# A runtime bound from row squares on ScalarE in place of Gram matrices on TensorE, with its last steps at another place and the whole order written anew

## The chip, the cores and the metric

The kernel runs on one core of a Trainium2 chip. The metric is the device time of one execution in microseconds (us), the median over runs. A core has five engines that run their own instruction queues in order: TensorE (PE; its weight loads are listed apart as PEld), VectorE (DVE), ScalarE (ACT), GpSimd (POOL), and SyncE (SP), which here issues the DMA transfers. [...]

## The reference, cut to what matters

Block-sparse attention over 4 batches, 8 heads, 768 positions and 64 columns a head, then an MLP whose activation is h times cos(h):

```python
def _attn_ref(q, k, v, sampled_blocks):
    scores = scale * np.matmul(q, k.transpose(0, 1, 3, 2))
    mask = np.abs(blk_i - blk_j) <= window           # own block and its neighbours, 32 positions a block
    mask = mask | (blk_i == 0) | (blk_j == 0) | (blk_i == n_blocks - 1) | (blk_j == n_blocks - 1)
    # and 3 drawn blocks for each block of queries
    scores = np.where(mask, scores, -1000000000.0)
    attn = np.exp(scores - np.max(scores, axis=-1, keepdims=True))
    attn = attn / (np.sum(attn, axis=-1, keepdims=True) + 1e-09)
    return np.matmul(attn, v)

def _moe_ref(x, w_in, w_out):      # x: 3072 x 512, w_in: 512 x 2048, w_out: 2048 x 512
    h = x @ w_in
    g = h * np.cos(h)
    return g @ w_out
```

## The kernel before, in words

**Tiling.** A batch has six query tiles of 128 rows: five sparse ones and one dense one (first and last block of the sequence among its rows). So there are 24 tiles, n = 0 to 23. Two tiles make one block of the MLP, m = 0 to 11.

**Attention, `attend(n)`.** For each unit of heads: scores on PE (`qk`, lines L1345 and L1356), masked maximum on DVE (`mx`, L1371), exponential on ACT (`ex`, L1393), a split of the result into a high and a low f16 part (`ph` on ACT, L1410; `pl` on DVE, L1414), a transpose by DMA into the tile PT (`PT`, L1434), and the product with V on PE (`pv`, L1445 and L1460). When all heads of a tile are there, DVE normalises into an f32 tile from the four `ot` buffers (`no`, L1482), ACT and DVE split it into f16 halves (`xh`, L1484; `xl`, L1486), and a DMA transposes these into `xT` (L1489). For one early tile PE transposes instead.

**MLP, `feed_forward(m)`.** 16 groups of 12 matmuls make h (`m{m}_{p}_{c}`, the first projection, L1626), ACT takes the cosine straight from PSUM (`sin`, L1643), DVE multiplies (`gm`, L1649), ACT and DVE split (`gh`, L1711; `gl`, L1714), and 16 groups of 6 matmuls make the output (`d{m}_{p}_{t}_{half}`, the second projection, L1723). ACT scales it out of PSUM (`o`, L1742) and SP stores it (`st`, L1747).

**The bound.** The sine table is used without reducing its argument, which is only right while h stays small. So the kernel works out a bound on h as it runs. Before the change each block m of x gives a Gram matrix on PE: 8 matmuls of 128x128 on `xT` (`xg{m}`, `x_gram`, L1658) into one of the two `ph` buffers in PSUM, which the first projection uses too. DVE takes its largest entry (`xr{m}`, `x_norm`, L1661). At the very end DVE scales and reduces these (`ba`, `bound_a`, L1667 and L1668), PE spreads the result over the partitions with one matmul (`bs`, L1113), and DVE multiplies by the weights' norms and compares (`bb`, `bound_b`, L1116 and L1674 to L1678). All five engines then load this flag into a register (L1681) and branch (L1769): over a second, general program that follows in the instruction stream, or into it. On these inputs the general program isn't run.

**Order.** A planner (`plan_kernel`) creates 3327 operations, each with its engine and its reads and writes. The table `POS` gives each its place: operations are issued in the order of these numbers, one in-order queue for each engine, with buffers handed out in that same order. So the table decides what stands behind what on every engine. With it stand `PARAMS` and the nominal costs, which decide nothing while the table covers every operation.

Of the kernel before, what the change touches and what calls it, by code (L numbers as in the profile page):

```python
# [16 lines left out]
ALU = mybir.AluOpType  # L17
# [3 lines left out]
P = 128  # L21
# [174 lines left out]
]  # L196


# [1611 lines left out]
```

## Time and profile before

| | |
|---|---|
| median of 3 runs | 787.79 us (785.78 to 788.1) |
| the profiled execution's own time | 788.36 us |
| its span, first to last instruction | 786.6 us |
| PE busy | 678.8 us (86%) |
| ACT busy | 597.9 us (76%) |
| DVE busy | 565.0 us (72%) |
| mean share of the 16 DMA engines, queue q1 | 85.5% |

Busy shares are averages over stages with different limits. A line of a group names the source line, the engine, the operation, what it writes and reads with shapes, a count, the busy time, the mean of one in ns, and after the second bar the idle time of that engine just before these instructions, with what ended it. A row of stages has the stretch, its length, then the busy us of PE, PEld, DVE, ACT and POOL with the number of instructions in brackets, TensorE's granted clock, the DMA engines' share and GB/s. A line of waits names who waited, for whom, and then the total, the number of times and the longest. The chain of waits follows the work that ended last back from the end, in order of time.

### The profile page before, as it was taken

Reading aid. Unit: us, or ns where it says so; the run is one execution under the profiler, and the core shown is the slowest. Engines: PE = TensorE matmul, PEld = TensorE weight load, DVE = VectorE, ACT = ScalarE, POOL = GpSimd, SP = SyncE. Lnnn points to the kernel's source line nnn. Section 1 sums busy time; section 2 is a strip of 40 time slices with the busy share of each in tenths; the row PEclk is TensorE's granted clock in tenths of the full one; section 3 lists DMA queues with packets and bytes.
Section 4 is the critical chain, followed back from the end, with each engine's and each line's share of the span. In section 5 each row is a group of like instructions: output and inputs, shape, how many; then the busy total and the mean of one; then the engine's idle time right before and its main releaser. Section 6 shows DMA issues by size and latency. Waiting matters only on the chain.

```text
span 786.6 us, 26927 instructions
## 1 busy us (share of the span) xinstructions
PE 678.8 (86%) x10953; PEld 473.1 (60%) x10953; DVE 565.0 (72%) x1646; ACT 597.9 (76%) x1216; POOL 17.1 (2%) x42
## 2 busy tenths in 40 slices
PE   2354459788998898999999999999999899999995
PEld 2333347566576556666676667667667576766762
DVE  5999989889788787757986677767874655464222
ACT  1867788889958988979888889878998666675321
POOL 5300000000000000000000000000000000000000
PEclk9855559999999999999999999999999999999998
DMA  9899997989999999998998999998998968644100
GB/s 311 251 275 223 188 263 172 199 205 213 256 187 215 170 183 186 176 212 186 201 181 199 197 184 195 229 184 141 185 190 176 171 128 177 120 83 78 54 1 31
DMA packets 243572, 141.11 MB, mean 179 GB/s; under 512 B 203376, under 2 KB 203504, under 8 KB 243440
## 3 DMA queue, kind: packets, MB, share of 16 engines
q1 hardware_dynamic: 243440, 139.32, 85.5%
q8 instruction: 87, 1.43, 0.8%
q14 instruction: 45, 0.37, 0.2%
HBM read 77.67 MB, written 12.58 MB: 115 GB/s over the span
## 4 chain that ended last, share of the span: by engine, by line
PE 40%; DVE 18%; DMA 17%; ACT 12%; issue 6%; SPq 6%; DVEq 1%; ACTq 0%
PE ph L1626 17%; PE po L1723 16%; DMA PT<-ring 5%; ACT P L1393 3%; DMA W<-kn 3%; DMA V<-scr 3%; DVE P L1371 3%; DVE ring L1414 2%; PE sp L1345 2%; SPq L1307 2%; DMA w<-in_moe_w_out_dram 2%; PE xp L1445 2%; ACT ring L1410 2%; DMA w<-in_moe_w_in_dram 1%; DMA U<-n 1%
## 5 line engine op out<-in xcount | busy, mean ns | idle before, releaser
L1626 PE MATMUL ph<-xT,w 128*128 128x256 f16 x2304 | 270.1, 275 | 4.7 <-DMA xT<-n 2.7
L1723 PE MATMUL po<-w,g 128*128 128x512 f16 x1152 | 263.7, 379 | 5.5 <-issue 2.9
L1626 PEld LDWEIGHTS <-w 128*128 128x128 f16 x2304 | 224.0, 99 | 44.2 <-DMA xT<-n 3.7
L1723 PEld LDWEIGHTS <-g 128*128 128x128 f16 x1152 | 110.4, 98 | 125.4 <-issue 5.4
L1393 ACT ACTIVATE P<-P,sm 128x256 f32<-128x256 f32 (+1 forms) x224 | 139.2, 622 | 19.0 <-DVE sm L1388 13.0
L1414 DVE TENSOR_TENSOR ring<-P,ring 128x512 f16<-128x512 f32 (+1 forms) x144 | 87.8, 625 | 37.7 <-ACT ring L1410 36.7
L1643 ACT ACTIVATE g<-ph,sm 128x512 f32<-128x512 f32 x96 | 72.3, 773 | 41.7 <-PE ph L1626 41.2
L1649 DVE SCALAR_TENSOR_TENSOR hs<-ph,sm,g 128x512 f32<-128x512 f32 x80 | 58.7, 747 | 50.4 <-ACT g L1643 50.0
L1410 ACT CAST ring<-P 128x512 f16<-128x512 f32 (+1 forms) x144 | 78.2, 566 | 15.5 <-DMA PT<-ring 13.7
L1345 PE MATMUL sp<-W,U 128*32 128x192 f16 (+1 forms) x2560 | 57.9, 240 | 23.4 <-DVE sm L1371 11.1
L1714 DVE TENSOR_TENSOR g<-hs,g 128x1024 f16<-128x1024 f32 x48 | 58.6, 1221 | 21.5 <-ACT g L1711 21.5
L1371 DVE CUSTOM_DVE_ANT_1 P<-sp,bias 128x256 f32<-128x256 f32 x160 | 61.8, 419 | 16.5 <-PE sp L1345 15.1
L1345 PEld LDWEIGHTS <-U 128*32 128x32 f16 x2560 | 45.8, 106 | 38.6 <-issue 29.8
L1711 ACT ACTIVATE g<-hs 128x1024 f16<-128x1024 f32 x48 | 50.4, 1051 | 12.5 <-DVE hs L1649 12.0
L1445 PE MATMUL xp<-V,PT 128*32 128x64 f16 x3840 | 41.5, 201 | 14.5 <-DMA PT<-ring 6.2
L1445 PEld LDWEIGHTS <-PT 128*32 128x32 f16 x3840 | 36.9, 97 | 24.2 <-issue 14.6
L1393 ACT ACTIVATION_READ_ACCUMULATOR P<-P,sm 128x1 f32 x224 | 41.8, 187 | 0.0
L1643 ACT ACT_TABLE_LOAD x30 | 38.5, 1283 | 0.5
L1371 DVE CUSTOM_DVE_ANT_1 P<-sp,dbias 128x384 f32<-128x384 f32 x64 | 34.4, 548 | 5.7 <-PE sp L1356 4.7
L1393 ACT ACT_TABLE_LOAD x29 | 37.2, 1283 | 0.9 <-DVE sm L1388 0.4
L1174 ACT COPY W<-W 128x256 f16 (+1 forms) x112 | 33.8, 377 | 5.3 <-issue 3.3
L1356 PE MATMUL sp<-W,U 128*128 128x384 f16 x128 | 29.6, 329 | 2.7 <-DVE sm L1371 2.2
(155 smaller groups left out, 644.5 us busy)
## 6 DMA issues: line engine op xcount, KB each, us to landing
V<-scr SPq DMA_DIRECT2D x40, 384.0 KB, 5.0
V<-scr SPq DMA_DIRECT2D x240, 64.0 KB, 3.5
w<-in_moe_w_in_dram SPq DMA_DIRECT2D x12, 512.0 KB, 6.0
stage<-in_k_dram SPq DMA_DIRECT2D x12, 512.0 KB, 6.2
w<-in_moe_w_out_dram SPq DMA_DIRECT2D x12, 512.0 KB, 6.7
V<-scr SPq DMA_DIRECT2D x8, 768.0 KB, 6.7
scr<-n SPq DMA_DIRECT2D x21, 256.0 KB, 3.9
qs<-in_q_dram SPq DMA_DIRECT2D x20, 256.0 KB, 3.9
```

What stands on the lines that cost most here:

```text
L1345: mm(o, U[:, z, h, rows], k, start=(a == 0 and z == 0 and part == 0), stop=(a == 1 and z == 1 and part == 1), tile_position=(0, BLK * j),)
L1371: self.nc.vector.tensor_tensor_reduce(out=self.head_cols(n, a, Pt).rearrange("p (n c) -> p n c", c=BLK), in0=self.head_cols(n, a, sp).rear ...
L1393: self.nc.scalar.activation(Pv, Pv, AF.Exp, scale=qc[:, 4:5], bias=nb[:, bcol : bcol + 1], accum_out=sums[:, 2 * j + a : 2 * j + a + 1],)
L1410: self.nc.scalar.copy(hi, p)
L1414: self.nc.vector.tensor_tensor(lo, p, hi, ALU.subtract)
L1445: mm(xp[32 * j : 32 * j + 32, h, :], PT[:, 4 * a + 2 * l + c, 32 * j : 32 * j + 32], V[:, j, c, h, d0:d1], start=(a == 0 and c == 0 and x ...
L1626: self.nc.tensor.matmul(ph[:, ff, :], self.W1[p][:, wl, cc, c * P : (c + 1) * P], xT[:, xl * NCC + cc, :], start=(j == 0), stop=(j == len( ...
L1643: self.nc.scalar.activation(self.half_cols(g, h), ph.rearrange("p f t -> p (f t)"), AF.Sin, scale=self.turns[b][:, p : p + 1], bias=self.h ...
L1649: self.nc.vector.scalar_tensor_tensor(self.half_cols(hs, h), ph.rearrange("p f t -> p (f t)"), c, self.half_cols(g, h), op0=ALU.mult, op1= ...
L1711: self.nc.scalar.activation(g[:, 0:1024], hs, AF.Copy)
L1714: self.nc.vector.tensor_tensor(g[:, 1024:2048], hs, g[:, 0:1024], ALU.subtract)
L1723: self.nc.tensor.matmul(po, g[:, gl, ff, t * P : (t + 1) * P], self.W2[p][:, wl, ff, :], start=(first and ff == half * hf and j == 0), sto ...
```

## The change

Instead of the Gram matrices, ACT squares each normalised f32 tile as soon as the order lets it, and adds along the row (`xs{n}`, `x_square`, 24 of them, one column each). The steps `ba`, `bs` and `bb` keep their arithmetic, on 6 columns a batch in place of 3. The order table is replaced as a whole: 3327 numbers again, since 24 operations go and 24 come. Two of its lines stand here.

```diff
 POS = [
-    2, 3, 5, 16, 4, 15, 9, 11, 10, 6, 39, 32, 46, 29, 48, 40, 49, 52, 57, 59, 60, 61, 62, 126, 245, 351, 154, 272, 353, 329, 73, 1091, 327, 956, 1387,
+    5, 8, 26, 9, 24, 144, 6, 7, 23, 25, 101, 10, 18, 11, 27, 12, 28, 29, 31, 32, 34, 35, 36, 180, 43, 456, 191, 62, 281, 160, 37, 976, 226, 1276,
...
     xTs = {}
+    xgs = []
...
         op("ACT", 0.525, np_ + 0.01, lambda: f(3), r=[y], w=[(xn, 0)], name=f"xh{n}")
+        if not general:
+            xgs.append(Val())
+            op("ACT", 0.613, np_ + 0.02, lambda: e.x_square(n, y.t), r=[y], w=[xgs[-1]], name=f"xs{n}")
         op("DVE", 0.602, np_ + 0.01, lambda: f(4), r=[y, (xn, 0)], w=[(xn, 1)], name=f"xl{n}")
...
-    xgs = []
-
     def feed_forward(m):
         b = seq[m * TT][0]
-        if not general:
-            gr, xg = Val("ph"), Val()
-            xgs.append(xg)
-            op("PE", 0.46, m * TT * CYC, lambda: e.x_gram(xTs[m].t, gr.t), r=[xTs[m]], w=[gr], name=f"xg{m}")
-            op("DVE", 0.21, m * TT * CYC, lambda: e.x_norm(m, gr.t), r=[gr], w=[xg], name=f"xr{m}")
...
-        self.xnorm = self.col(len(self.seq) // self.TT)
+        self.xnorm = self.col(len(self.seq))
...
-    def x_gram(self, xT, g):
-        n = self.TT * self.NCC
-        for k in range(n):
-            r, c = divmod(k, self.NCC)
-            x = xT[:, c, r * P : r * P + P]
-            self.nc.tensor.matmul(self.gram_view(g), x, x, start=(k == 0), stop=(k == n - 1))
-
-    def x_norm(self, m, g):
-        self.nc.vector.tensor_reduce(self.xnorm[:, m : m + 1], self.gram_view(g), AX.X, ALU.max)
+    def x_square(self, n, y):
+        self.square(self.xnorm[:, n : n + 1], y)

     def bound_a(self):
-        nc, n = self.nc, len(self.seq) // self.TT // self.B
+        nc, n = self.nc, len(self.seq) // self.B
```

`square` is `activation(junk, src, Square, accum_out=acc)`, the same helper (L1068) that squares q and the later k and v tiles.

Three places of the new order matter below. The first is DVE's end of the program. In the version before, behind the last block's products and splits (L1649, L1714), stand the last Gram reduction and the steps `ba` and `bb`:

```order
L1649 SCALAR_TENSOR_TENSOR hs_81<-ph_116,sm,g_84 128x512
L1714 TENSOR_TENSOR g_84<-hs_81,g_84 128x1024
L1661 TENSOR_REDUCE sm<-ph_117 128x1
L1667 TENSOR_SCALAR sm<-sm 128x3 x4
L1668 TENSOR_REDUCE sm<-sm 128x1
L1116 TENSOR_REDUCE sm<-sp_112 128x1
L1674 TENSOR_TENSOR sm<-sm 128x1
L1676 TENSOR_TENSOR sm<-sm 128x1 x2
L1677 TENSOR_SCALAR sm<-sm 128x1
L1678 TENSOR_SCALAR sm<-sm 128x1
L1681 TENSOR_LOAD sm
L1769 COMPARE_AND_BRANCH
```

Of the changed kernel, DVE at the place where the last tile is normalised (there L1479 is `no23`, L1483 `xl23`, L1657 and L1658 `ba`, L1113 to L1668 `bb`, L1646 the last block's products; the numbers are three to ten lower than before):

```order
L1704 TENSOR_TENSOR g_84<-hs_81,g_84 128x1024
L1477 RECIPROCAL sm<-sm 128x8
L1479 TENSOR_TENSOR ot_108<-xp_115,sm 128x512
L1483 TENSOR_TENSOR n_89<-ot_108,n_89 128x512
L1657 TENSOR_SCALAR sm<-sm 128x6 x4
L1658 TENSOR_REDUCE sm<-sm 128x1
L1113 TENSOR_REDUCE sm<-sp_112 128x1
L1664 TENSOR_TENSOR sm<-sm 128x1
L1666 TENSOR_TENSOR sm<-sm 128x1 x2
L1667 TENSOR_SCALAR sm<-sm 128x1
L1668 TENSOR_SCALAR sm<-sm 128x1
L1646 SCALAR_TENSOR_TENSOR hs_82<-ph_116,sm,g_85 128x512
```

`ba` and `bb` moved from behind the last split of the program to ahead of all products of the last block. On PE the matmul `bs` moved with them: from the last row of the program to a place with 6 groups of the second projection of m = 10 and the whole of m = 11 (16 and 16 groups) still behind it, and 3 groups of 6 matmuls between it and `pv23_5`, the last product with V.

ACT at the same place, in the version before (L1484 is `xh23`, L1711 `gh`, L1742 the outputs of m = 10):

```order
L1643 ACTIVATE g_84<-ph_116,sm 128x512
L1484 CAST n_90<-ot_109 128x512
L1711 ACTIVATE g_84<-hs_81 128x1024
L1742 ACTIVATE ot_110<-po_119,sm 128x512
L1742 ACTIVATE ot_108<-po_118,sm 128x512
```

and in the changed one (L1481 is `xh23`, L1065 the squares of tiles 22 and 23, L1701 `gh`):

```order
L1640 ACTIVATE g_84<-ph_117,sm 128x512
L1701 ACTIVATE g_84<-hs_81 128x1024
L1481 CAST n_89<-ot_108 128x512
L1065 ACTIVATE junk,sm<-ot_111 128x512
L1065 ACTIVATE junk,sm<-ot_108 128x512
L1732 ACTIVATE ot_109<-po_119,sm 128x512
```

Two squares now stand between `xh23` and the outputs of m = 10, and `ba` waits for the second of them.

SP's last rows before, where ot_109 is tile 23 (stored in two parts) and the last ot_110 is tile 22:

```order
L1747 DMA out_dram<-ot_111 128x512
L1747 DMA out_dram<-ot_109 96x512
L1747 DMA out_dram<-ot_109 32x512
L1747 DMA out_dram<-ot_110 128x512
L1681 TENSOR_LOAD sm
L1769 COMPARE_AND_BRANCH
```

and now, where ot_108 is tile 22 and ot_110 tile 23:

```order
L1737 DMA out_dram<-ot_109 128x512
L1737 DMA out_dram<-ot_108 128x512
L1737 DMA out_dram<-ot_110 96x512
L1737 DMA out_dram<-ot_110 32x512
L1671 TENSOR_LOAD sm
L1759 COMPARE_AND_BRANCH
```

The tile with two stores is now the last one, so SP issues two transfers and not one behind the last output.

## Rows read from the trace of the kernel before

**Rows 1.** Busy time by stage: length; engines; granted TensorE clock, DMA share, GB/s.
```profile
0.00:140.00 140.00, 73.73 (x1634) 57.96 (x1635) 125.07 (x345) 97.76 (x204) 17.06 (x42) 0.70 0.92 241
140.00:640.00 500.00, 466.87 (x7808) 321.71 (x7807) 376.23 (x1160) 422.69 (x888) 0.00 (x0) 1.00 0.98 190
640.00:740.00 100.00, 100.00 (x1258) 68.60 (x1257) 51.36 (x120) 66.58 (x112) 0.00 (x0) 1.00 0.57 116
740.00:778.00 38.00, 37.93 (x258) 24.69 (x255) 10.13 (x13) 10.70 (x13) 0.00 (x0) 1.00 0.03 7
```

**Rows 2.** Waits of PE, 140 to 778 us: total, times, longest.
```profile
PE xp L1445 <- DMA V<-scr: 3.4, 4, 2.2
PE xp L1460 <- DMA PT<-ring: 3.0, 4, 1.3
...
PE ph L1626 <- DVE sm L1661: 0.5, 1, 0.5
```

**Rows 3.** End of the chain of waits: start, us, what.
```profile
765.82 11.65 PE po L1723 x54
777.48 0.46 PE ph L1658 x8
...
778.25 0.78 DVE sm L1667 x4
...
779.28 0.24 PE sp L1113
...
780.58 0.15 DVE sm L1678
```

**Rows 4.** The flag's load, line L1681: ns, first and last start.
```profile
L1681 SPq TENSOR_LOAD <-sm x1: 279/279/279, 780.8 to 780.8; - x1
```

**Rows 5.** The branch, line L1769, and the semaphore steps behind it.
```profile
L1769 SPq EVENT_SEMAPHORE  x9: 17/17/17, 784.2 to 784.8; - x9
L1769 PEldq COMPARE_BRANCH  x1: 4177/4177/4177, 781.4 to 781.4; - x1
L1769 PEldq EVENT_SEMAPHORE  x1: 51/51/51, 785.6 to 785.6; - x1
```

**Rows 6.** Tile ot, 770 to 787 us: the last outputs and stores.
```profile
L1747 SPq DMA_DIRECT2D out_dram<-ot x3: 332/350/426, 774.3 to 778.2; - x3
L1742 ACT ACTIVATE ot<-po,sm x2: 687/687/687, 773.6 to 777.5; 128x512 f32<-128x512 f32 x2
```

**Rows 7.** Groups by line: the parts that go.
```profile
L1658 PE MATMUL ph<-xT 128*128 128x128 f16 x96 | 7.3, 219 | 0.1
L1661 DVE TENSOR_REDUCE sm<-ph 128x1 f32<-128x128 f32 x12 | 3.4, 284 | 7.5 <-PE ph L1658 7.5
```

**Rows 8.** Line L1658, 640 to 700 us.
```profile
L1658 PE MATMUL ph<-xT x8: 219/219/220, 699.4 to 699.8; 128*128 128x128 f16 x8
```

**Rows 9.** ACT in order of time: a square of 128x512 and its neighbours.
```profile
311.88 0.62 ACT L1068 ACTIVATE junk<-stage 128x512 bf16<-128x512 f32 x1
...
312.49 0.76 ACT L1643 ACTIVATE g<-ph,sm 128x512 f32<-128x512 f32 x1
```

**Rows 10.** Groups by line: all loads of ACT's function tables.
```profile
L1643 ACT ACT_TABLE_LOAD x30 | 38.5, 1283 | 0.5
L1393 ACT ACT_TABLE_LOAD x29 | 37.2, 1283 | 0.9 <-DVE sm L1388 0.4
L1068 ACT ACT_TABLE_LOAD x1 | 1.3, 1283 | 0.7 <-PEq L1786 0.7
```

**Rows 11.** Line L1484, the high half of every tile: ns, first and last start.
```profile
L1484 ACT CAST n<-ot x24: 601/617/621, 91.7 to 727.5; 128x512 f16<-128x512 f32 x24
```

**Rows 12.** Sum over 160 to 200, 250 to 300 and 550 to 600 us.
```profile
sum 140.00, PE 130.96 PEld 91.50 DVE 113.79 ACT 128.93 POOL 0.00; mean PE 43.65 PEld 30.50 DVE 37.93 ACT 42.98 POOL 0.00
```

**Rows 13.** In order of time: PE behind the last product with V, and xh23.
```profile
726.57 9.23 PE L1723 MATMUL po<-w,g 128*128 128x512 f16 x42
...
727.50 0.62 ACT L1484 CAST n<-ot 128x512 f16<-128x512 f32 x1 [4.21 <-DVE ot L1482]
```

More of the change, by code (lines that the diff above doesn't have):

```diff
@@ L871 @@
     KD, KX = 384, 1152
-    SMALL = 296 + 72 + 24
+    SMALL = 296 + 72 + 40
     kv = wc = None
```

260 rows, old and new, of the table POS are left out of this document.

## The prediction

> **What bounds the kernel now.** I read the busy time by stage first [rows 1]. Up to 140 us PE works 73.73 us of 140 while DVE works 125.07: the start hangs on DVE and on what feeds it. From 140 to 640 PE has 466.87 of 500, ACT 422.69, and the DMA engines are taken to 0.98; three resources lie close together, and PE is idle for 33.1 us in all. From 640 to 778 PE has no idle time to speak of (100.00 of 100, then 37.93 of 38). So the end is set by PE's work, except where in the first 640 us something else leaves it idle. Next I read what PE waits for between 140 and 778 us [rows 2]: small pieces, the two largest groups 3.4 and 3.0 us, both on DMAs of the attention. Last I read the end of the chain of waits [rows 3]: the second projection ends at 777.48 us, then come the last Gram matrix and a string of small DVE steps up to the flag at 780.73, and only then the flag's loads and the branch [rows 4, 5]. The span ends at 786.6, 9.12 us behind the last useful matmul.
>
> **The tail.** Before, the flag is loaded from 780.8 on, SP's load being the row shown [rows 4]; PE's branch starts at 781.4 and takes 4.18 us, its semaphore step stands at 785.6 [rows 5], and 1.0 us later the span ends. SP is a little quicker: from its load at 780.8 to its last semaphore step at 784.8 are 4.0 us. In the changed kernel the flag is there long before, and each engine goes to its load when its own queue is through. With T for the end of the last matmul: ACT's output takes 0.69 us, and SP has two stores behind it, 0.35 and 0.33 us [rows 6], with some 0.1 us between them, so SP's load starts at T + 1.45 and its last step is at T + 5.45. PE's load starts at T, its step at T + 4.8. With the same 1.0 us behind the later one the span ends at T + 6.45. Against 9.12 that is **−2.6 us**, the last Gram matrix (0.46 us) within it. What stays is the branch, which no edit touches.
>
> The row shows 4.18 us for PE's branch and nearly as long from SP's load to its steps [rows 4, 5]. [...] I go by the rows.
>
> **The Gram matrices in the body.** 96 matmuls go [rows 7]. In the chain 8 of them take 0.46 us [rows 3], so the other eleven are 11 x 0.46 = 5.1 us. Only one of the eleven lies behind 640 us, where PE is full [rows 8]; the other ten lie where PE has idle time to swallow them. I take all of it, **−5.1 us**, since most of that idle time is short waits inside a full queue; the lower bound is one, −0.5 us. With them goes their hold on one of the two PSUM buffers of the first projection, which cost PE one wait of 0.5 us on DVE's reduction [rows 2]: **−0.5 us**. The 12 reductions themselves free 3.4 us of DVE [rows 7], which is under 80% busy behind 140 us [rows 1]; I count nothing, and at most those 3.4.
>
> **The squares.** A square of this size holds ACT's queue, with the read of its accumulator, for 0.61 us, from its start to that of the next instruction [rows 9]; 24 are 14.6 us. Counted in the two orders, the loads of ACT's tables fall from 60 to 58, 2 x 1.28 us [rows 10]: 12.1 us net. From 140 to 640 ACT is idle for 77.3 us [rows 1], which can hide them all; nothing hides them where ACT is nearly full. A tile is finished every (727.5 − 91.7) / 23 = 27.6 us [rows 11]. The three fullest stretches make 140 us, with ACT busy for 128.9 of them, 92% [rows 12], so 140 / 27.6 = 5.1 squares fall there: 5.1 x 0.61 = **+3.1 us**. The bounds are 0 and 12.1. Behind each square wait the exponentials and the cosines, and behind those DVE and PE.
>
> A square also keeps one of the four ot buffers until it has run, and the squares of tiles 0 and 1 stand far behind in ACT's new order. I cost this at nothing, because the other buffers cover it; if they don't, the nearest row is PE's longest single wait in the first group, 2.2 us [rows 2].
>
> **The wait that is added.** The matmul `bs` now stands in the middle of PE's queue, with everything of m = 11 behind it, so each us it waits is a us of the end. It needs `ba`, which needs the squares of tiles 22 and 23. From where PE turns from the last product with V to other work, 726.57, to the start of `xh23`, 727.50, DVE's product between them, are 0.93 us, `xh23` takes 0.62 [rows 13], the two squares 1.22, and from `ba` to the spreading matmul it is 779.28 − 778.25 = 1.03 [rows 3]: 3.8 us. PE has 18 matmuls to do in between, at 11.65 / 54 us each [rows 3]: 3.9 us. So it is just covered; with the matmul's own 0.24 us [rows 3] and a little lateness **+0.5 us**. The bounds are 0.2 and, without cover, 4.0.
>
> **The order.** All 3327 numbers are new. What that does the rows of before can't show. They bound it: the two largest groups of PE's waits, 6.4 us [rows 2], can be lost or come once more. I take 0 and keep ±6.4. The first 140 us are in this too, since nothing else of the change acts there.
>
> **The sum.** −2.6 − 5.1 − 0.5 + 3.1 + 0.5 = −4.6 us. It is made against the profiled execution, 788.36 us (1.8 us more than its span), and gives 783.8 there. That execution lies 0.6 us above the median of 787.79, so I forecast **783.2 us**.
>
> **Rivals.**
> - *The attention sets the pace up to 640 us.* DMA at 0.98 speaks for it, and PE's largest waits are on DMAs. Then the ten early Gram matrices only become idle time of PE, and the squares hide too: 787.79 − 2.6 − 0.5 (the Gram matrix at 699) + 0.5 = 785.2. Against it: PE is 93% busy there.
> - *ACT becomes the bound* (slower). Place: 140 to 640 us, where ACT is 85% busy and every square stands in one queue with exponentials and cosines. Price: all 12.1 us reach the end, −2.6 − 5.1 − 0.5 + 0.5 + 12.1 = +4.4, so 792.2. It makes the kernel slower than before once more than 7.7 / 0.61, about 13 squares, delay the end. For it: the 92% of the three stretches. Against it: 77.3 us idle, and two loads fewer.
> - *The new order is better or worse than the old by itself.* 783.2 ± 6.4: 776.8 or 789.6. For it: all is moved. Against it: the parts that the rows can follow, near the end, are laid out with about the same covers.
> - *The flag is not ready in time*, so `bs` holds PE as long as the old tail took: 783.2 + 2.6 = 785.8. The 3.8 us against 3.9 speak for it, the bound of 4.0 against much more.
> - *The squares switch ACT's tables.* 24 loads of 1.28 us would be 31 us more, some 814. The rows show loads at the cosine and the exponential, and a single one at the squares' line [rows 10], whose squares of q, k and v stand all through the program; the order holds two loads fewer. [...]
>
> **How the numbers follow.** The forecast 0.42, with its own range of 780 to 785.4; the attention's pace 0.18; ACT as the bound 0.13; the order worse 0.14, better 0.10; the flag late 0.02; the tables 0.01. A measurement of this kernel tells about 0.3% from no change, 2.4 us: below 785.4 is faster, above 790.2 slower. Faster: 0.42, half of the attention's case (it lies on the edge), and 0.10, together 0.61. Same: the other 0.09, 0.10 of the worse order, 0.02 of the late flag and 0.01 of ACT's case, 0.22. Slower: 0.12 of ACT's case, 0.04 of the order's, 0.01 for the tables, 0.17. The range reaches from 777.0 (no square on the path and half of 6.4 won: 783.2 − 3.1 − 3.2) to 790.5, which takes in the worse order whole and leaves most of ACT's case out.
>
> **What would show it.** The tail: the distance from the last second projection to the end of the span should be 6.5 us, with no DVE step in it. The body: PE's busy time should fall by about 7 us, and its idle time between 140 and 640 us stay near 33; if that idle time grows by 5 us, the attention sets the pace. ACT: 24 squares at 0.61 us, 58 loads, and no stretch at which PE waits longer for a cosine or exponential; ACT above 95% over a stretch would show the second rival. `bs`: a wait of PE at that matmul under half a us. The start: the first product of the first projection at about the same time; a shift of some us there is the order's doing. The forecast is wrong if the last matmul doesn't end some 2 us or more ahead of 777.48.

## The result and the profile after

The changed kernel takes 781.73 us (median of 8 runs, 778.12 to 783.65) against 788.51 us for the kernel before, run beside it (8 runs, 785.78 to 792.12): a ratio of 0.9904, with a 95% interval of 0.9876 to 0.9932. The interval lies below 1, so the changed kernel is faster, by 0.7 to 1.2%. The forecast was 783.2 us, 4.6 less than before; the profiled executions stand at 782.21 and 788.36, 6.2 apart, and their spans at 780.4 and 786.6. Ratios, here and below, leave out executions in the chip's slower state, one of which (827.1 us) is in the median given for e5. Line numbers of the changed kernel are 3 to 10 lower: L1623 is the first projection, L1713 the second, L1442 and L1457 the products with V, L1110 the spreading matmul, L1671 the flag's load, L1759 the branch.

Busy time by stage in the changed kernel, with the columns of [rows 1], the last stretch up to the end of the second projection:

```profile
0.00:140.00 140.00, 70.65 (x1623) 56.81 (x1624) 124.14 (x345) 97.63 (x207) 15.32 (x42) 0.73 0.93 244
140.00:640.00 500.00, 467.14 (x7784) 319.72 (x7783) 378.32 (x1158) 430.09 (x925) 0.00 (x0) 1.00 0.97 191
640.00:740.00 100.00, 100.00 (x1243) 68.92 (x1242) 50.18 (x122) 70.58 (x122) 0.00 (x0) 1.00 0.53 106
740.00:774.00 34.00, 33.50 (x214) 20.57 (x211) 9.22 (x10) 8.56 (x11) 0.00 (x0) 1.00 0.01 4
```

PE is idle for 69.35 us in the start (66.27 before), for 32.86 us from 140 to 640 (33.13 before) and not at all behind that. The first product of the first projection starts at 119.0 us in place of 116.9. The end of the chain of waits, and then the flag's load, the branch and the stores by line (ns, first and last start):

```profile
752.78 20.73 PE po L1713 x96
773.51 0.02 issue
773.54 0.69 ACT ot L1732
```

```profile
L1671 PEldq TENSOR_LOAD <-sm x1: 489/489/489, 769.5 to 769.5; - x1
...
L1671 SPq TENSOR_LOAD <-sm x1: 579/579/579, 775.1 to 775.1; - x1
...
L1759 SPq EVENT_SEMAPHORE  x9: 17/17/17, 778.5 to 779.1; - x9
...
L1759 PEldq COMPARE_BRANCH  x1: 3421/3421/3421, 770.1 to 770.1; - x1
L1759 PEldq EVENT_SEMAPHORE  x1: 51/51/51, 773.5 to 773.5; - x1
...
L1737 SPq DMA_DIRECT2D out_dram<-ot x3: 332/332/418, 773.0 to 774.6; - x3
```

The second projection ends at 773.51 us, 3.97 earlier than in [rows 3], and the span ends 6.89 us behind it in place of 9.12. No DVE step stands there any more. PE's load (769.5) and its branch (770.1) lie ahead of 773.51: its instruction queue runs on while the last matmuls are still at work. SP, with its stores ahead of it, is the last.

The squares and ACT's table loads by line, and the spreading matmul:

```profile
L1640 ACT ACT_TABLE_LOAD x29 | 37.2, 1283 | 0.5
...
L1390 ACT ACT_TABLE_LOAD x28 | 35.9, 1283 | 0.4
...
L1065 ACT ACTIVATE junk<-ot 128x512 bf16<-128x512 f32 x24 | 14.9, 620 | 0.2
...
L1065 ACT ACT_TABLE_LOAD x1 | 1.3, 1283 | 0.7 <-PEq L1776 0.7
```

```profile
L1110 PE MATMUL sp<-ident,sm x1: 219/219/219, 723.8 to 723.8; 128*128 128x128 f16 x1
its engine sat idle before it (us, times) until:
who waited for it (us, times):
  DVE sm L1113: 0.7, 1
```

24 squares of 0.62 us, 58 loads, and no idle time of PE ahead of the spreading matmul. The high half of the tiles starts later and ends earlier than in [rows 11], at 99.0 against 91.7 us and at 720.9 against 727.5.

### The profile page after: what moved, and what is told of

Its sections match the earlier page's. It is cut to its first block, busy times and chain, and to the rows that moved or that the text cites. A ratio compares the mean times of both kernels' runs of the same rounds, so it can differ in the third digit from the quotient of the medians.

```text
span 780.4 us, 26779 instructions
## 1 busy us (share of the span) xinstructions
PE 671.3 (86%) x10857; PEld 466.0 (60%) x10857; DVE 561.9 (72%) x1634; ACT 607.1 (78%) x1262; POOL 15.3 (2%) x42
## 3 DMA queue, kind: packets, MB, share of 16 engines
q8 instruction: 87, 1.43, 0.8%
## 4 chain that ended last, share of the span: by engine, by line
PE 38%; DVE 19%; DMA 19%; ACT 13%; issue 6%; SPq 4%; DVEq 0%; ACTq 0%
PE ph L1623 16%; PE po L1713 15%; DMA PT<-ring 8%; ACT P L1390 4%; DVE ring L1411 3%; DMA W<-kn 2%; DVE P L1368 2%; DMA qs<-in_q_dram 2%; PE sp L1342 2%; PE xp L1442 2%; ACT ring L1407 2%; SPq L1304 2%; DMA U<-n 2%; PE sp L1353 1%; DVE hs L1646 1%
## 5 line engine op out<-in xcount | busy, mean ns | idle before, releaser
L1623 PE MATMUL ph<-xT,w 128*128 128x256 f16 x2304 | 267.4, 273 | 6.6 <-DVE hs L1646 4.4
L1713 PE MATMUL po<-w,g 128*128 128x512 f16 x1152 | 265.7, 381 | 4.1 <-issue 3.8
L1623 PEld LDWEIGHTS <-w 128*128 128x128 f16 x2304 | 223.2, 98 | 46.7 <-issue 8.5
L1713 PEld LDWEIGHTS <-g 128*128 128x128 f16 x1152 | 109.6, 98 | 126.4 <-issue 7.2
L1646 DVE SCALAR_TENSOR_TENSOR hs<-ph,sm,g 128x512 f32<-128x512 f32 x80 | 59.4, 747 | 47.3 <-ACT g L1640 46.4
L1342 PE MATMUL sp<-W,U 128*32 128x64 f16 (+1 forms) x2560 | 55.5, 238 | 30.1 <-DVE sm L1368 20.1
L1342 PEld LDWEIGHTS <-U 128*32 128x32 f16 x2560 | 44.0, 104 | 45.0 <-issue 39.9
L1704 DVE TENSOR_TENSOR g<-hs,g 128x1024 f16<-128x1024 f32 x48 | 58.6, 1220 | 14.1 <-ACT g L1701 13.7
L1701 ACT ACTIVATE g<-hs 128x1024 f16<-128x1024 f32 x48 | 50.3, 1049 | 13.6 <-DVE hs L1646 13.6
L1442 PE MATMUL xp<-V,PT 128*32 128x64 f16 x3840 | 40.8, 199 | 4.0 <-DMA PT<-ring 1.9
L1442 PEld LDWEIGHTS <-PT 128*32 128x32 f16 x3840 | 36.4, 96 | 13.0 <-issue 8.9
L1732 ACT ACTIVATE ot<-po,sm 128x512 f32<-128x512 f32 x20 | 13.4, 677 | 33.6 <-PE po L1713 33.6
```

The lines of the kernel that those rows point to most:

```text
L1342: mm(o, U[:, z, h, rows], k, start=(a == 0 and z == 0 and part == 0), stop=(a == 1 and z == 1 and part == 1), tile_position=(0, BLK * j),)
L1442: mm(xp[32 * j : 32 * j + 32, h, :], PT[:, 4 * a + 2 * l + c, 32 * j : 32 * j + 32], V[:, j, c, h, d0:d1], start=(a == 0 and c == 0 and x ...
L1623: self.nc.tensor.matmul(ph[:, ff, :], self.W1[p][:, wl, cc, c * P : (c + 1) * P], xT[:, xl * NCC + cc, :], start=(j == 0), stop=(j == len( ...
L1646: self.nc.vector.scalar_tensor_tensor(self.half_cols(hs, h), ph.rearrange("p f t -> p (f t)"), c, self.half_cols(g, h), op0=ALU.mult, op1= ...
L1701: self.nc.scalar.activation(g[:, 0:1024], hs, AF.Copy)
L1704: self.nc.vector.tensor_tensor(g[:, 1024:2048], hs, g[:, 0:1024], ALU.subtract)
```

## The experiments

The kernel before, run beside each group of four, stood at 787.93 (e1 to e4), 788.47 (e5 to e8) and 790.01 us (e9 to e12); ratios are to it, and kernels of different groups are compared by their ratios.

My theory was that the Gram matrices come off PE one for one, that the squares hide, and that the early flag shortens the tail, each by itself. The rival was that only the new order makes this possible. The first four kernels try the parts in the other's order. An edit of the order is written with the names of the operations: a line with + stands at its new place.

**e1: the squares in the order of before.**

```diff
 xh0
+xs0            (so for all 24 tiles; the Gram matrices and reductions go)
 xl0
 ...
 the last output, then ba, bs, bb
```

> The squares replace the Gram matrices, but the order of before is kept: each square stands right behind the tile's high half on ScalarE, and the flag is still made at the very end. Theory (the Gram matrices' time on TensorE comes off the end one for one, and the squares hide in ScalarE's idle time): TensorE's busy time falls by about 7 us, its idle time between 140 and 640 us stays within 3 us of 33, the start stays as before, the last second projection ends at about 772, and the tail behind it is some 7.5 us because the last reduction no longer waits for a Gram matrix: 788.5 - 5 - 2 = 781.5. Rival (the new order made the gain, the freed TensorE time is swallowed by waits): 786 to 789. Rival (squares cost what they occupy on ScalarE, 14.6 us): 793 or more.

Measured: 808.67 us, ratio 1.0266 [1.0219, 1.0313]. A plain miss: PE has less to do, and the kernel is 21 us slower. It doesn't wait for ACT: the waits from 140 to 780 us that the profile puts down to ACT are 0.8 us in sum (1.0 in the kernel before). The largest group and one small one of its kind are these:

```profile
PE xp L1442 <- issue: 25.4, 9, 5.1
...
PE sp L1342 <- issue: 0.4, 1, 0.4
```

"issue" is time in which the engine waits for nothing that the profile shows. The timeline of PE at one of the nine (start, us, what, and in brackets the idle time ahead):

```profile
475.10 2.75 PE L1713 MATMUL po<-w,g 128*128 128x512 f16 x12
477.78 1.47 PE L1442 MATMUL xp<-V,PT 128*32 128x64 f16 x158
483.85 0.67 PE L1442 MATMUL xp<-V,PT 128*32 128x64 f16 x34 [4.60 <-issue]
```

PE stops in the middle of one operation of 192 equal matmuls, behind number 158, with all its data there. What ends there is a block of PE's instructions, as the queue that brings them shows (an instruction block, not one of the MLP's blocks m). The page's row of that queue (packets, MB):

```profile
q8 instruction: 87, 1.43, 0.8%
```

1.43 MB in 87 packets are 16,384 bytes each; 10,857 weight loads, as many matmuls and the semaphore steps, some 21,800 instructions, fill 87 packets at 256 each (22,272 places). Numbering PE's instructions in the trace, I find all nine waits at one place of the count: 193 or 194 above a multiple of 256. At the one shown, the block before was entered at 477.97 and used up in 1.07 us by 128 small load-and-matmul pairs; the next one's packet landed at 482.39, 4.42 us behind that entry, and PE went on 1.46 us later. Of the 77 blocks from 100 to 775 us 60 last 6 us or more, and none of these shows such a wait; the nine, and two more at 106.6 and 269.3 us, stand behind shorter blocks. This fits an engine that has hardly more than the next block at hand (my reading of these landings; how much it holds no run shows by itself): a block that lies inside a burst of small products is used up before the one after it has come. A Gram matrix was 16 instructions: without the twelve, every block end lies up to 192 instructions away from its old place in the order.

**e2: e1 with the last steps of the bound ahead of the last second projection.**

```diff
 d10_3_1_1
+bs             (ba behind gl10_3, bb behind bs)
 d10_3_0_0
```

> As e1, and the flag's last steps are put ahead of the last block of the second projection in the old order too. Theory: half a microsecond to 1 us better than e1 (about 781), because without a Gram matrix the flag is anyway ready about 1.5 us behind the last matmul, and the two stores of SyncE take as long. Rival (the early flag is worth the whole 2 to 3 us of tail): 2.5 us better than e1.

Measured: 802.87 us, ratio 1.0198 [1.0149, 1.0247], a miss for the same reason. Between the last matmul and the end of the span lie 6.3 us against 7.3 in e1.

**e3: the kernel before, with only its last Gram matrix and the flag moved.**

```diff
 d10_3_0_1
+xg11, xr11, ba
 m11_2_0
 ...
 m11_1_1
+bs, bb
```

> The kernel before with its Gram matrices and its order; only the last Gram matrix, its reduction and the last steps of the flag stand ahead of the last block's first projections. Theory: the tail behind the last second projection falls from 9.1 to about 6.7 us and nothing else changes: the last matmul some 0.7 us later for the Gram matrix and the spreading matmul ahead of it, so 788.5 - 1.7 = 786.8. Rival (the tail's gain needs the squares, since the last Gram matrix waits for the last transposed tile and holds TensorE): 788 to 789.

Measured: 785.89 us, ratio 0.9972 [0.9940, 1.0003]. The last matmul ends at 777.09 us (777.48 before) and the span 6.01 us behind it (9.12): in the trace the tail's gain stands alone, without squares and without a new order. The time by itself doesn't show it: the interval reaches just over 1. Its end of the chain:

```profile
765.42 11.67 PE po L1723 x54
777.09 0.02 issue
777.12 0.69 ACT ot L1742
```

**e4: the changed kernel's order with the Gram matrices back.**

```diff
 d3_0_0_0
+xg3, xr3       (so for all blocks; the squares go)
 m3_2_0
```

> The new order with the Gram matrices put back into it (each some place behind the first group of its block's second projection, the last one and the flag's steps ahead of the last block), and no squares. Theory: TensorE's busy time and the end both grow by about 7 us against the changed kernel: 788 to 789. Rival (the new order made the gain): 782 to 784. If a Gram matrix's hold on a PSUM buffer makes the first projection wait at these places, the waits on its reduction will show it, and the time is over 790.

Measured: 801.41 us, ratio 1.0163 [1.0116, 1.0211], 12 to 13 us above what was expected. Twelve operations of 0.46 us don't cost 20. Its waits of PE from 140 us on:

```profile
PE xp L1445 <- issue: 15.5, 6, 4.6
...
PE ph L1626 <- issue: 3.4, 3, 2.1
...
PE po L1723 <- issue: 0.8, 1, 0.8
```

Either order loses its time when its count of PE instructions is changed, and either is good with the count it came with. The next three kernels change the count and nothing else that matters.

**e5: the changed kernel with instructions that do nothing useful.**

```diff
+        for _ in range(30 if self.nk == 4 else 0):
+            self.nc.tensor.transpose(out=tp[:, 0], in_=self.ident, identity=self.ident)
         for h in range(self.H):
             self.nc.tensor.transpose(out=tp[:, h], in_=kn[:, h], identity=self.ident)
```

> The changed kernel with 60 transposes of the identity (60 loads and 60 matmuls of TensorE, 120 instructions) put in two lots into gaps of the start in which TensorE waits for data (29 to 34.7 and 35.6 to 41.7 us). Nothing else is changed. Theory (TensorE's instructions come in blocks of 256, and a block that is used up faster than the next one arrives makes TensorE wait): all later block ends move by 120 instructions, out of the places that the shipped order leaves them in. Laid out on the issue times of the changed kernel, with about 5.3 us as the least time from one block's start to the next, the waits grow by up to 34 us: 803 to 815 us, with PE waits marked issue of over 20 us between 140 and 780. Rival (the old order lost its 20 us to ScalarE's queue, where the squares stand behind other work): the order of the work is that of the changed kernel, so 781.7 to 784.

Measured: 801.2 us, ratio 1.0149 [1.0086, 1.0212] against 0.9904 for the changed kernel; 16 us by the profile's last matmul (789.38 against 773.51). The loss is there, but below the expected lower end of 803. From 50 to 138 us its instructions run some 0.8 to 1.3 us earlier than in the changed kernel, so the added transposes cost nothing where they stand. Then:

```profile
PE xp L1448 <- issue: 18.6, 8, 3.8
PE sp L1348 <- issue: 5.6, 2, 3.4
```

**e6: e1 with 56 such transposes**, 112 instructions, ahead of the same two operations.

```diff
+        for _ in range(28 if self.nk == 4 else 0):
+            self.nc.tensor.transpose(out=tp[:, 0], in_=self.ident, identity=self.ident)
```

> The squares in the order of the kernel before (e1, 808.7 us) with 56 such transposes (112 instructions) in the same two gaps. Theory: the block ends move, for this order to the shift that laid out the same way gives the least waits (27 us in place of 44): 788 to 796, that is work added and 12 to 20 us faster than e1. Rival (squares in ScalarE's queue): 808 to 811.

Measured: 783.28 us, ratio 0.9928 [0.9902, 0.9954]. Work is added and 25 us go, more than expected. At 133 us e6 is 2.6 us ahead of e1, at the last matmul 23.5, so it isn't the start that is won. PE's waits from 140 us on:

```profile
PE xp L1448 <- issue: 8.4, 4, 3.5
...
PE po L1719 <- issue: 4.4, 2, 2.5
...
PE ph L1629 <- issue: 1.9, 2, 1.5
```

**e7: e1 with a stand-in of 8 small pairs for each Gram matrix**, so that the count is that of before.

```diff
+            x = xT[:, c, r * P : r * P + 8]
+            self.nc.tensor.matmul(self.gram_view(g)[0:8, 0:8], x, x, start=(k == 0), stop=(k == n - 1))
```

> The squares in the order of the kernel before, and in place of each Gram matrix 8 loads of 8 columns and 8 matmuls of 8 columns, whose result nothing reads: TensorE's instruction count stays that of the kernel before everywhere, so the block ends do too. The flag's steps stand at the very end. Theory: the waits marked issue return to about 8 us and the time to 782 to 787 (the small pairs give back part of the 0.46 us that each Gram matrix took). Rival (squares or order cost the 20 us in e1): 802 to 810.

Measured: 784.85 us, ratio 0.9956 [0.9930, 0.9982], as expected. The waits are back to those of before:

```profile
PE po L1724 <- issue: 0.8, 1, 0.8
...
PE xp L1446 <- issue: 0.7, 1, 0.7
```

These three settle it: with the same useful work in the same order, 120 instructions more make the changed kernel 16 us slower (last matmul), and 112 more make e1 25 us faster. ScalarE's queue, the rival, has the same instructions in the same order in e1, e6 and e7. And e7's pairs stand where the Gram matrices stood, all through the program, and not in the start, so it isn't the place of the added work either. The waits of over 0.4 us at the end of a block that lasted less than 6 us, from 100 to 775 us, counted in each trace from the start of one weight load to the next, beside the end of the last second projection and the median (the traced execution of e2 took 810.24 us, 7 more than its median; the others lie within 3.3 us of theirs):

```
                          waits, us  times   last matmul   median
before                       8.4       3       777.5      788.5
after                        6.6       4       773.5      781.7
e1 old order                31.5      11       800.7      808.7
e2 old order, early         30.0      11       802.2      802.9
e3 Gram matrices, early     11.5       7       777.1      785.9
e4 Gram matrices, new       25.2      12       796.1      801.4
e5 after + 120              30.5      13       789.4      801.2
e6 old order + 112          18.7       9       777.2      783.3
e7 old order, small pairs    9.5       4       773.2      784.9
e12 old order, early + 114  17.6      10       774.1      783.1
```

Where data came late at the same place, the profile names what brought it and not "issue" (e7's last one, 3.6 us at 611.6, goes under ACT).

The waits don't turn into time one for one: e5's are 24 us above the changed kernel's and its last matmul comes 16 us later; e6's are 13 below e1's and its last matmul comes 23.5 earlier. PE's busy time tells more. From 140 us to the last second projection each of the four does 9233 to 9241 matmuls. In the changed kernel PE is busy for 600.6 us of this stretch and idle for 32.9; in e1 611.2 and 49.5, in e5 607.9 and 41.5, in e6 602.9 and 34.3. So between e1 and e6 15.2 us are idle time and 8.4 are matmuls that take longer; between the changed kernel and e5 it is 8.7 and 7.2. The granted clock goes with the second part. Two stages of e1, with the columns of [rows 1]:

```profile
140.00:640.00 500.00, 456.41 (x7448) 312.43 (x7447) 366.21 (x1118) 423.53 (x903) 0.00 (x0) 0.97 0.92 186
640.00:740.00 100.00, 94.13 (x1368) 64.46 (x1367) 53.91 (x141) 72.15 (x135) 0.00 (x0) 0.98 0.58 113
```

Both means are 1.00 in the changed kernel. The clock records of the traces have two levels, a granted clock of 0.50 and of 1.00; PE is at the lower one for 30.7 us of that stretch in e1, 20.5 in e5, 13.7 in e6 and 3.4 in the changed kernel and in e7. In e1 six of seven falls of the clock, in e5 five of six, lie inside a wait at a block's end or at most 1.2 us behind one. In the changed kernel it is so once: PE goes on at 612.85 us behind a wait of 3.34, the clock is at 0.50 from 613.66 to 617.06, and some 9 matmuls of the second projection take these 3.40 us, where 24 take 4.90 at 1.00 (617.1 to 622). I take it that the idle time of the waits brings the clock down; no run shows the cause by itself. That e5's 24 us of waits add only 8.7 us of idle time means that many of them fall where PE would have waited for data.

**e8: the changed kernel without the squares.**

```diff
     def x_square(self, n, y):
-        self.square(self.xnorm[:, n : n + 1], y)
+        pass
```

> The changed kernel without the 24 squares (the bound on x is a constant, so that part of the computation is left out); TensorE's instructions are the same. Theory (the squares lie beside other work but for three stretches where ScalarE is full): 779.5 to 782.0, 0 to 2 us less than the changed kernel. Rival (ScalarE became the bound of the body): 775 or less.

Measured: 783.53 us, ratio 0.9957 [0.9928, 0.9986], against 0.9904 for the changed kernel: above what was expected and no gain. So the squares cost nothing that can be seen. Why the time is rather longer isn't shown.

**e9: each square twice.**

```diff
         self.square(self.xnorm[:, n : n + 1], y)
+        self.square(self.xnorm[:, n : n + 1], y)
```

> The changed kernel with each of the 24 squares taken twice (14.9 us more of ScalarE). Theory (most squares lie beside waits of ScalarE, some of them in stretches where it is full): 782 to 788, at most a third of the added 15 us shows. Rival (ScalarE sets the pace of the body): 793 or more.

Measured: 786.58 us, ratio 0.998 [0.9947, 1.0013], within the range that was expected. By the ratios it is 0.76%, 6 us, behind the changed kernel, a little over the third of the added 15 us that was to show at most; the traced executions lie 2.8 us apart. So ACT doesn't set the pace, but twice the squares aren't free. In its trace the last second projection ends 2.2 us later (775.66), 1.0 of which is this wait behind 640 us:

```profile
PE sp L1110 <- DVE sm L1659: 1.0, 1, 1.0
```

That is the wait that the change adds: with two more squares, of the last two tiles, the spreading matmul comes too late. In the changed kernel it stood at 0.

**e10: the changed kernel with the last steps of the bound at the very end.**

```diff
-ba, bs, bb at their places
+ba, bs, bb behind the last second projection
```

> The changed kernel with the bound's last steps (ba, bs, bb) put at the very end of every engine's order, behind the last second projection. TensorE's instruction count ahead of it is less by one pair only. Theory: the last square is long done, so the flag is ready about 1.5 us after the last matmul and the branches follow: 782 to 784, 0 to 2 us behind the changed kernel. Rival (the place of the last steps carries most of the gain): 784 to 787.

Measured: 785.07 us, ratio 0.9971 [0.9935, 1.0006], the rival's figure. The chain behind the last matmul, and the branch:

```profile
755.94 20.72 PE po L1713 x96
776.66 0.07 PE sp L1110
...
777.78 0.15 DVE sm L1668
```

```profile
L1759 SPq EVENT_SEMAPHORE  x9: 17/17/17, 782.1 to 782.7; - x9
...
L1759 PEldq COMPARE_BRANCH  x1: 4221/4221/4221, 778.9 to 778.9; - x1
L1759 PEldq EVENT_SEMAPHORE  x1: 51/51/51, 783.2 to 783.2; - x1
```

The span ends 7.54 us behind the last matmul (6.89 in the changed kernel): the late flag's own price is 0.65 us in these two traces. PE's branch of 4.2 us, which lay beside the last matmuls, stands behind them again. The other 3.15 us lie ahead of the flag, in work whose order is the same; the waits at block ends are 9.6 us there against 6.6, one of them (1.5 us at 456) without a counterpart in the changed kernel's trace, and the clock is at its lower level, 0.50, for 10.2 us behind 140 against 3.4. That the late flag caused these isn't shown.

**e11: the changed kernel with its start in the order of before.**

```diff
-first 890 places: order of the changed kernel
+the same operations in the order of before, then xs2, xs3, xs0
```

> The order of the changed kernel, with the operations of its first 890 places (to about 140 us) put among each other in the order of the kernel before; the sets of instructions ahead of and behind that place are the same, so the block ends behind it stay. Theory (the start of the changed kernel lost 3 us by its order, the rest gained): 778 to 781.5. Rival (the start's loss is made up by the later order, or the start of before is only good with what follows it there): 782 to 786.

Measured: 795.68 us, ratio 1.0107 [1.0049, 1.0166], a miss. Up to 140 us PE gets through as many matmuls, 1623; at the 5000th PE instruction, at 205 us in the changed kernel, it is 12.9 us behind, and stays 12 to 17 behind. Two stretches there:

```profile
180.00:195.00 15.00, 13.71 (x148) 10.30 (x146) 9.65 (x32) 11.77 (x27) 0.00 (x0) 0.91 0.83 159
195.00:210.00 15.00, 13.08 (x98) 7.73 (x94) 8.10 (x21) 9.15 (x21) 0.00 (x0) 0.89 0.60 140
```

The granted clock is 0.91 and 0.89 there, behind 9.2 us of PE's idle time in 135 to 180 (3.1 in the changed kernel). One 2.8 us wait at a block's end stands at its head, and the three squares left over stand in its chain at 163 to 166 us. Which of these begins it stays open. So the start of before isn't better ahead of the new order: it makes the kernel 14 us slower.

**e12: e2 with 57 transposes**, a try for a better kernel.

```diff
+        for _ in range(28 if self.nk == 4 else 0):      (and 29 at the other place)
+            self.nc.tensor.transpose(out=tp[:, 0], in_=self.ident, identity=self.ident)
```

> e2 (the squares in the order of the kernel before, the bound's last steps ahead of the last second projection; 802.9 us) with 57 transposes of the identity in the gaps of the start, as in e6. Theory: the block ends move as in e6, and the early flag takes 2 us more off: 779 to 783. Rival (the early flag's instructions put the block ends back, or the pads help by delaying the start): 784 or more.

Measured: 783.06 us, ratio 0.9933 [0.9902, 0.9965], at the edge of what was expected and 20 us better than e2. It doesn't beat the changed kernel (0.9904), and no other kernel here does.

## Why the prediction was right, and which of its terms were not

In the traces the changed kernel is 6.2 us faster, where 4.6 were forecast. The two large terms that make it faster, the tail and the Gram matrices, were right in place and size. The rest came out near by luck in part: the squares' +3.1 didn't come, a start that came out 1.1 us worse than the terms say made up for some of it, and the new order, which I had taken as neutral, was needed.

- **The tail** (−2.6 us forecast): 9.12 to 6.89 us, −2.2. SP's load starts 1.6 us behind the last matmul (T + 1.45 was forecast), its last step 5.6 behind (5.45), and the span ends 1.3 us after that, not 1.0. PE's branch is no longer a bound at all: I had put its load at T, and it stands 4.0 us ahead of T. e3 shows the tail's gain apart from the rest. The long branch is PE's alone, 4177 ns before the change and 3421 after. SP's compare was short before the change too:

```profile
L1769 SPq COMPARE_BRANCH  x1: 53/53/53, 781.1 to 781.1; - x1
```

What takes SP's time lies behind it, up to its first step: 3.1 us before (781.1 to 784.2) and 2.7 after (775.8, again 53 ns, to 778.5). No run here shows what that is.

- **The Gram matrices** (−5.1): they came off one for one. PE's idle time between 140 and 640 us stayed, 33.1 and 32.9, which was the test set for it; the attention's pace, as a rival, would have made it grow by 5. Behind 140 us lie ten Gram matrices of 0.46 us ahead of the last second projection, 4.6 us, and three second-projection matmuls more to do than before (below), 0.6 us; the difference of the two is the 4.0 us by which the last matmul comes earlier. PE's busy time up to the last matmul fell by more than 5.1, from 777.5 − 99.4 = 678.1 us to 773.5 − 102.2 = 671.3: the rest is in the start. The wait for the PSUM buffer (−0.5) is gone with the reduction that held it, too small to be seen in the sum.
- **The squares** (+3.1): 0. The term was over-sized: I let every square in a stretch with ACT at 92% count in full. e8 shows no gain without them, and of 15 us more in e9 some 6 reach the end by the ratios. The tables were loaded 58 times, as counted.
- **The added wait** (+0.5): 0 in the trace, and e9 shows how near it was.
- **The start** (within the order's 0): at 140 us PE has done the same matmuls in both traces, but for the eight of a Gram matrix (0.61 us there) and three of the second projection (22 before, 19 after, 0.63 us). So the changed kernel is 0.6 us behind there, and has gained nothing from that Gram matrix. Its 3.1 us more of idle time are not 3.1 us lost: 1.8 us of them are the same matmuls taking less time, at a granted clock of 0.73 against 0.70. Tail, ten Gram matrices and start make −2.2 − 4.6 + 0.6 = −6.2 us, the difference of the spans.
- **The order** (0, ±6.4): here the reasoning failed, though the sum did not. I treated the order as noise around parts that work by themselves. They don't: squares in the old order are 2.0 to 2.7% slower than the kernel before (e1, e2), Gram matrices in the new one 1.6% (e4). The new order keeps PE's block ends out of the bursts once 192 instructions are gone (6.6 us of waits, against 31.5 in e1); the transposes of e6 and e12 do nearly as well in the old one. I took the waits of PE marked "issue" before, 3.8 us from 140 to 778, for a remainder without a cause:

```profile
PE po L1723 <- issue: 2.9, 1, 2.9
...
PE xp L1445 <- issue: 0.7, 1, 0.7
```

They were the one sign of it. The bound of ±6.4 was taken from PE's waits on DMAs and couldn't contain it.

The issue times of the traces let one lay the blocks out at every other count. I took 5.3 us as the least time from one block's entry to the next, an estimate from e1, where at the eleven waits it was 1.8 to 6.4 us (1.07 + 4.80 at the one shown). The shortfall, summed from 100 to 770 us, is then 12.3 us for the changed kernel where it stands and 11.8 to 46.8 over all shifts, for the kernel before 17.7 and 13.4 to 58.2, for e1 43.7 and 26.9 to 52.7. These estimates are too high: the waits counted above are 6.6, 8.4 and 31.5. But they rank the three, and by them both shipped orders stand close to their own best shift. From this layout the number of transposes in e5, e6 and e12 was chosen.

## What to carry to other kernels

When an edit removes or adds instructions on an engine that issues short ones in bursts, count them (here 120 more cost 16 us in one order, and 112 more won 25 in the other): look where its waits marked "issue" stand, and whether they lie a fixed number of instructions apart. Look at the granted clock behind such waits too: between e1 and e6, 8.4 us were matmuls that ran slower, beside 15.2 us of idle time. A gain on such an engine should be tried with the instruction count padded back to its old value, or shifted in a few steps, before an order is judged. And when a result rests on a new order and a new operation together, run each in the other's absence: here each half alone was 13 to 21 us slower than the kernel before, and the two together 7 faster.

## What the runs showed of the hardware

PE's instructions came in packets of 16,384 bytes, 256 instructions each by the count in e1. At the eleven waits of e1 the missing packet landed 0.5 to 4.9 us after the block ahead of it was entered, and its first instruction ran 1.2 to 1.6 us after that. Of the 77 blocks of e1 from 100 to 775 us, the 60 that lasted 6 us or more show no such wait; the eleven waits, 31.5 us, stand behind blocks that were used up in 1.07 to 3.46 us.

In the changed kernel PE's load of the flag started 4.0 us and its branch 3.4 us ahead of the end of its last matmul. The branch, of 3421 ns, cost nothing there: PE's semaphore step stands at 773.5 us, SP's last at 779.1. In this trace and in the one before the change a packet of PE's instructions lands during the branch, and PE's semaphore step follows 1.5 us behind it (772.0 and 773.5; 784.1 and 785.6).
